# SwiGLU gate and up projections by Strassen's seven products over two token halves, with left sides made a tile ahead

## The chip, the cores and the metric

The kernel runs on one core of a Trainium2 chip. The metric is the device time of one execution in microseconds (us). A run is one execution; one more execution is recorded by the hardware profiler, and all lines of the profile come from it. The engines are PE (matrix multiplications, with its weight loads as PEld), DVE (VectorE), ACT (ScalarE), POOL (GpSimd) and SP (which here only issues transfers). Each works through its own queue of instructions in the order written and waits for others by semaphores.

## The reference

The input `x` holds 4096 tokens of 640 values. A first half (a layer norm, a Fourier transform over the tokens, two small complex matrices for each of four blocks, a shrinkage, the inverse transform, a gate) is added to `x`. The second half is the one that changes:

```python
h = _layernorm(x, axis=-1) * (1 + cb) + sb
# _B_ref(h, w_gate, w_up, w_down):
g = _silu(h @ w_gate)          # 640 x 1728
u = h @ w_up                   # 640 x 1728
x = x + gb * ((g * u) @ w_down)   # 1728 x 640
```

`cb`, `sb` and `gb` are rows of a modulation vector, and all data are float32.

## The kernel before

Every matrix product is made from two rounded parts of each factor, a high part of 12 bits and the rest: `high*high + high*low + low*high`, so three matmuls in place of one. ACT makes the high part with a copy to the rounded type, and DVE the low part with a subtraction. Everywhere below "split" means these two instructions.

The first half of the network fills the first 330 us. The last step of its inverse transform, which takes the rows `s2` from DRAM, is done in the second part: for a row of 128 tokens, `pre_c` (L991) loads and splits the spectrum row, `pre_a` (L1000) makes six matmuls of 320 columns with the matrix `gt`, adds the gated result to `x2` and takes the layer norm's statistics, `pre_x` (L1017) normalizes, and `pre_b` (L1024) transposes to `ht`, the left side with the 640 features on partitions as five slices of 128, split.

The feed-forward part runs over eight tiles of 512 tokens. For each tile:

- `split_weights` (L1037) loads 128 columns of `w_gate` or `w_up` (five slices of the 640 features) and splits them, two units ahead of their use.
- `unit` (L1094) has 27 steps: a gate and an up step for each of 13 chunks of 128 hidden features, and one for the remaining 64 of both. `proj` (L1047) makes 5 x 3 matmuls of 512 columns into one PSUM bank. A gate step ends with ACT's Silu (L1107) from the bank. An up step ends with DVE's product (L1119), and a split of it (L1120 and L1121) that gives `ah`, the left side of the down projection. No bank is added to again once it has been read.
- `down` (L1123) runs in two passes over the hidden chunks (7, then 6 and the rest), each time for four groups of 128 tokens and two halves of 320 columns. The split down weights `wdh`, `wdl` stay in SBUF throughout. A pass ends with DVE's product with the gate `gbb` (L1147) and the addition to `x2` (L1148).
- The next tile's rows are loaded and prepared between units 16 and 26, and transposed between the groups of the second pass.

The order of all instructions is written out by hand (`manual_schedule`), so the order in the text is the order of every engine's queue. Weights and rows are loaded by SP, the matrices `gt` by POOL, and outputs are stored by ACT's queue. PSUM has five names of banks, `b0`, `b1` with one bank each, and `p1`, `p2`, `p3` with two each.

Of the kernel before, what the change touches and what calls it, by code (L numbers as in the profile page):

```python
# [171 lines left out]
def body(tc, x, w1, b1, w2, b2, wg, wu, wd, c, wm, k_fa, k_tb, k_tx, k_bm, k_bx, k_ga, k_ge, k_id, out, dbg=None):  # L172
# [27 lines left out]
    with ExitStack() as top:  # L200
# [714 lines left out]

        with ExitStack() as ff:
            fp = ff.enter_context(tc.tile_pool(name="fp", bufs=1, reuse_waits="tile"))
            hts = {}
            gts = {}
            ahs = {}  # L920

            first = ExitStack()
            if dbg != "x2":
                first.enter_context(tc.manual_schedule())

            gbb = fp.tile([P, D], F32, name="gbb")
            early = {"wr": [fp.tile([P, 5, P], F32, tag="wr", bufs=4, name="wr0_0")],
                     "wh": [fp.tile([P, 5, P], F32R, tag="wh", bufs=3, name="wh0_0")]}
            gacc = fp.tile([P, D], F32, tag="chl", bufs=1, name="gacc")
            early["cr"] = [fp.tile([P, D], F32, tag="cr", bufs=2, name=f"gwm{k}") for k in range(2)]  # L930
            early["chh"] = [fp.tile([P, D], F32R, tag="chh", bufs=1, name="chh1_0")]
            wxh = fp.tile([P, D], F32R, name="wxh")
            early["wl"] = [fp.tile([P, 5, P], F32R, tag="wl", bufs=3, name="wl0_0")]
            early["xn2"] = [fp.tile([P, D], F32, tag="xn2", bufs=4, name="xn2_0_0")]
            hts[0] = fp.tile([P, 5, 2, 512], F32R, tag="ht", bufs=1, name="ht0")
            wxl = fp.tile([P, D], F32R, name="wxl")
            early["yo"] = [fp.tile([P, 320], F32, tag="yo", bufs=2, name="yo0")]
            wdh = fp.tile([P, NFC, D], F32R, name="wdh")
            wdl = fp.tile([P, NFC, D], F32R, name="wdl")

            def tile_of(shape, dt, tag, bufs, name):
                if early.get(tag):
                    return early[tag].pop(0)
                return fp.tile(shape, dt, tag=tag, bufs=bufs, name=name)


            wgv = wg.rearrange("(k p) f -> p k f", p=P)
            wuv = wu.rearrange("(k p) f -> p k f", p=P)

            gws = {}  # L950


            def gate_b(k):
                if k < 5:
                    gws[k] = tile_of([P, D], F32, "cr", 2, f"gwm{k}")
                    nc.sync.dma_start(gws[k], wm[:, 5, k, :])
                if k == 1:
                    dve.tensor_scalar(gacc, gws[0], sc[:, 0:1], None, op0=OP.mult)
                elif 1 < k < 6:
                    dve.scalar_tensor_tensor(gacc, gws[k - 1], sc[:, k - 1:k], gacc, op0=OP.mult, op1=OP.add)  # L960
                elif k == 6:
                    for hf in range(2):
                        pm = ps.tile([P, 512], F32, tag="p3", name=f"gpm{hf}")
                        mm(pm[:, :320], ones, gacc[:, 320 * hf:320 * hf + 320], start=True, stop=True)
                        act.activation(gbb[:, 320 * hf:320 * hf + 320], pm[:, :320], AF.Copy)

            def load_down(fc):
                wr = tile_of([P, D], F32, "wr", 4, f"wdr{fc}")
                if fc < NFC:
                    nc.sync.dma_start(wr, wd[128 * fc:128 * fc + 128, :])  # L970
                    h, l = wdh[:, fc, :], wdl[:, fc, :]
                else:
                    nc.sync.dma_start(wr[0:64], wd[128 * fc:F, :])
                    nc.sync.dma_start(wr[64:128], wd[128 * fc:F, :])
                    h, l = wxh, wxl
                act.activation(h, wr, AF.Copy)
                dve.tensor_tensor(l, wr, f32(h), op=OP.subtract)

            def pre_load(t):
                x2 = fx.tile([P, 4, D], F32, tag="gx", bufs=2, name=f"x2_{t}")  # L980
                nc.sync.dma_start(x2, xv[:, 4 * t:4 * t + 4, :])
                x2s[t] = x2
                gt = fp.tile([P, 4, 2, N1], F32R, tag="gt", bufs=1, name=f"gt{t}")
                pool.dma_start(gt.rearrange("p a b c -> p (a b c)"), k_ga[:, 1024 * t:1024 * t + 1024])
                gts[t] = gt
                xns[t] = []

            chs = {}
            mvs = {}

            def pre_c(t, i):  # L991
                cr = tile_of([P, D], F32, "cr", 2, f"cr{t}_{i}")
                nc.sync.dma_start(cr, s2[:, 4 * t + i, :])
                chh = tile_of([P, D], F32R, "chh", 1, f"chh{t}_{i}")
                chl = fp.tile([P, D], F32R, tag="chl", bufs=1, name=f"chl{t}_{i}")
                act.activation(chh, cr, AF.Copy)
                dve.tensor_tensor(chl, cr, f32(chh), op=OP.subtract)
                chs[t, i] = (chh, chl)

            def pre_a(t, i):  # L1000
                x2 = x2s[t]
                gt = gts[t]
                chh, chl = chs[t, i]
                for hf in range(2):
                    e = slice(320 * hf, 320 * hf + 320)
                    py = ps.tile([P, 512], F32, tag="p3", name=f"py{t}_{i}_{hf}")
                    mm(py[:, :320], gt[:, i, 0, :], chh[:, e], start=True, stop=False)
                    mm(py[:, :320], gt[:, i, 0, :], chl[:, e], start=False, stop=False)
                    mm(py[:, :320], gt[:, i, 1, :], chh[:, e], start=False, stop=True)
                    yg = tile_of([P, 320], F32, "yo", 2, f"yg{t}_{i}_{hf}")  # L1010
                    dve.tensor_tensor(yg, py[:, :320], gab[:, e], op=OP.mult)
                    dve.tensor_tensor(x2[:, i, e], x2[:, i, e], yg, op=OP.add)
                if dbg == "x2":
                    nc.sync.dma_start(ov[:, 4 * t + i, :], x2[:, i, :])
                mvs[t, i] = layer_stats(fp, x2[:, i:i + 1, :], 1, f"b{t}_{i}")

            def pre_x(t, i):  # L1017
                x2 = x2s[t]
                mv, rs = mvs[t, i]
                xn = tile_of([P, D], F32, "xn2", 4, f"xn2_{t}_{i}")  # L1020
                dve.tensor_scalar(xn, x2[:, i, :], mv[:, 0, 0:1], rs[:, 0:1], op0=OP.subtract, op1=OP.mult)
                xns[t].append(xn)

            def pre_b(t, k):  # L1024
                if k == 0 and t:
                    ht = fp.tile([P, 5, 2, 512], F32R, tag="ht", bufs=1, name=f"ht{t}")
                    hts[t] = ht
                ht = hts[t]
                pt = ps.tile([P, 512], F32, tag="p3", name=f"pt{t}_{k}")
                for i in range(4):  # L1030
                    pe.transpose(pt[:, 128 * i:128 * i + 128], xns[t][i][:, 128 * k:128 * k + 128], idn)  # L1031
# [5 lines left out]
            def split_weights(src_list, nm):  # L1037
                wr = tile_of([P, 5, P], F32, "wr", 4, f"wr{nm}")
                for dst, src in src_list:
                    nc.sync.dma_start(wr[:, :, dst], src)  # L1040
# [194 lines left out]
```

## Time and profile before

| What | Value |
|---|---|
| median of 3 runs | 1501.98 us (1499.21 to 1503.86) |
| the profiled execution: time, span | 1502.37 us, 1500.6 us |
| PE busy | 1456.5 us (97%), 8114 matmuls |
| DVE, ACT, POOL busy | 871.8, 587.7, 117.0 us (58%, 39%, 8%) |
| first transposes of the feed-forward part on PE | at 330.8 us |
| from 700 to 1100 us: PE, DVE, ACT busy | 400.0, 217.4, 114.0 us |
| moved by DMA | 179.92 MB, mean 120 GB/s |

The page gives for every group of equal instructions its busy time, the mean of one in ns, and the idle time of the engine just before them with what ended it. A view of waits adds up that idle time by who waited for whom. A timeline row gives start, duration, engine, line, operation, output and inputs, the shape, and in brackets an idle time before it with its releaser. The granted clock of PE over the span is 0.993 of full speed.

### The profile page before, as it was taken

The numbers are of one execution on the slowest core, as the hardware profiler recorded it, in microseconds if no ns is written. First come the engines' busy times: TensorE is split into PE (matmuls) and PEld (weight loads), VectorE is DVE, ScalarE is ACT, GpSimd is POOL, SyncE is SP. The second block draws the span as 40 slices with busy tenths as digits, with TensorE's granted clock in tenths as the row PEclk, the third lists the DMA queues.
The fourth block names the chain that finished last, engine by engine and source line by source line (L and its number), as shares of the span: only waits on it lengthen the run. The fifth ranks groups of instructions, "written<-read, shape, count | busy, mean of one in ns | idle before, by whom it ended". The sixth has DMA issues, their size and how long they took to land.

```text
span 1500.6 us, 20793 instructions
## 1 busy us (share of the span) xinstructions
PE 1456.5 (97%) x8114; PEld 1292.2 (86%) x8114; DVE 871.8 (58%) x1598; ACT 587.7 (39%) x1034; POOL 117.0 (8%) x215
## 2 busy tenths in 40 slices
PE   7599999989999999999999999999999999999998
PEld 2399999868989898989898989898889988898888
DVE  8478888877475437543844374447444744564433
ACT  7569989746232314231323132313231322223220
POOL 5400100030010001000100010001000100000000
PEclk9799999999999999999999999999999999999999
DMA  9946556647432423241324132513241324223210
GB/s 377 319 168 188 167 160 184 206 135 233 140 88 84 111 74 97 85 138 47 100 84 138 53 102 75 154 36 102 80 140 53 94 80 131 62 71 89 70 44 35
DMA packets 183057, 179.92 MB, mean 120 GB/s; under 512 B 19312, under 2 KB 153648, under 8 KB 180016
## 3 DMA queue, kind: packets, MB, share of 16 engines
q1 hardware_dynamic: 173728, 152.56, 34.0%
q0 software_dynamic: 3904, 14.91, 3.0%
q10 hardware_dynamic: 5328, 11.14, 2.0%
q8 instruction: 63, 1.03, 0.3%
q14 instruction: 34, 0.28, 0.1%
HBM read 137.95 MB, written 31.46 MB: 113 GB/s over the span
## 4 chain that ended last, share of the span: by engine, by line
PE 84%; DVE 5%; ACT 4%; DMA 4%; POOL 1%; SPq 1%; issue 1%; DVEq 0%; ACTq 0%; POOLq 0%
PE pd L1143 26%; PE pg L1050 8%; PE pg L1049 8%; PE pg L1051 8%; PE pu L1050 8%; PE pu L1049 8%; PE pu L1051 8%; PE pc L649 1%; PE pl L603 1%; PE pa L407 1%; DMA xx<-tt 1%; PE pb L542 1%; PE pt L1031 1%; DMA s<-xa 1%; DMA g<-s 1%
## 5 line engine op out<-in xcount | busy, mean ns | idle before, releaser
L1143 PE MATMUL pd<-wdh,ah 128*128 128x320 f32 x1664 | 384.4, 310 | 0.1
L1143 PEld LDWEIGHTS pd<-wdh,ah 128*128 128x128 f32 x1664 | 282.4, 188 | 1.0 <-DVE yo L1147 0.4
L1143 PE MATMUL pd<-wdl,ah 128*128 128x320 f32 x832 | 257.0, 309 | 0.0
L1044 DVE TENSOR_TENSOR wl<-wr,wh 128x640 fp32r<-128x640 f32 x216 | 177.5, 822 | 121.5 <-ACT wh L1043 121.5
L1050 PE MATMUL pg<-ht,wh 128*128 128x512 f32 x555 | 216.2, 389 | 0.0
L1049 PE MATMUL pg<-ht,wh 128*128 128x512 f32 x555 | 216.1, 389 | 0.0
L1051 PE MATMUL pg<-ht,wl 128*128 128x512 f32 x555 | 216.0, 389 | 0.0
L1049 PE MATMUL pu<-ht,wh 128*128 128x512 f32 x515 | 200.8, 390 | 0.0
L1050 PE MATMUL pu<-ht,wh 128*128 128x512 f32 x515 | 200.6, 390 | 0.0
L1051 PE MATMUL pu<-ht,wl 128*128 128x512 f32 x515 | 200.4, 389 | 0.0
L1107 ACT ACTIVATE sg<-pg 128x512 f32<-128x512 f32 x104 | 62.2, 598 | 336.2 <-PE pg L1051 335.3
L1120 ACT ACTIVATE ah<-sg 128x512 fp32r<-128x512 f32 x104 | 65.8, 632 | 295.4 <-DVE sg L1119 295.4
L1043 ACT ACTIVATE wh<-wr 128x640 fp32r<-128x640 f32 x216 | 157.1, 728 | 41.5 <-DVE x L1148 38.2
L1147 DVE TENSOR_TENSOR yo<-pd,gbb 128x320 f32<-128x320 f32 x128 | 62.7, 490 | 183.7 <-PE pd L1143 183.7
L1143 PEld LDWEIGHTS pd<-wdl,ah 128*128 128x128 f32 x832 | 156.3, 188 | 0.6
L1051 PEld LDWEIGHTS pg<-ht,wl 128*128 128x128 f32 x555 | 104.2, 188 | 21.8
L1119 DVE TENSOR_TENSOR sg<-pu,sg 128x512 f32<-128x512 f32 x104 | 71.7, 689 | 88.1 <-PE pu L1051 88.1
L1049 PEld LDWEIGHTS pg<-ht,wh 128*128 128x128 f32 x555 | 104.2, 188 | 21.0
L1050 PEld LDWEIGHTS pg<-ht,wh 128*128 128x128 f32 x555 | 104.2, 188 | 21.0
L1121 DVE TENSOR_TENSOR ah<-sg,ah 128x512 fp32r<-128x512 f32 x104 | 72.2, 694 | 72.7 <-ACT ah L1120 72.7
L1051 PEld LDWEIGHTS pu<-ht,wl 128*128 128x128 f32 x515 | 96.7, 188 | 20.3
L1049 PEld LDWEIGHTS pu<-ht,wh 128*128 128x128 f32 x515 | 96.7, 188 | 19.6
(209 smaller groups left out, 2001.6 us busy)
## 6 DMA issues: line engine op xcount, KB each, us to landing
wr<-in_B_w_gate_dram SPq DMA_DIRECT2D x104, 320.0 KB, 3.3
wr<-in_B_w_up_dram SPq DMA_DIRECT2D x104, 320.0 KB, 3.2
x<-in_A_x_dram SPq DMA_DIRECT2D x8, 1280.0 KB, 6.2
out_dram<-x ACTq DMA_DIRECT2D x31, 320.0 KB, 2.2
g<-s SPq DMA_DIRECT2D x28, 320.0 KB, 7.1
xx<-tt SPq DMA_DIRECT2D x56, 160.0 KB, 3.7
s<-co POOLq DMA_DIRECT2D x28, 320.0 KB, 3.4
cr<-s SPq DMA_DIRECT2D x28, 320.0 KB, 3.3
```

The lines of the kernel that those rows point to most:

```text
L407: mm(pa, fa, xnr[:, i, :, 0:128] if i < 4 else xnr[:, :, :, 128:160], start=True, stop=True)
L1043: act.activation(wh, wr, AF.Copy)
L1044: dve.tensor_tensor(wl, wr, f32(wh), op=OP.subtract)
L1049: mm(pp, wh[:, k, :], ht[:, k, 0, :], start=(k == 0), stop=False)
L1050: mm(pp, wh[:, k, :], ht[:, k, 1, :], start=False, stop=False)
L1051: mm(pp, wl[:, k, :], ht[:, k, 0, :], start=False, stop=(k == 4))
L1107: act.activation(sg, pg, AF.Silu)
L1119: dve.tensor_tensor(sg, pu, sg, op=OP.mult)
L1120: act.activation(ah[:, 0, :], sg, AF.Copy)
L1121: dve.tensor_tensor(ah[:, 1, :], sg, f32(ah[:, 0, :]), op=OP.subtract)
L1143: mm(pd[:, :320], l, m, start=(i == 0), stop=(i == len(seq) - 1))
L1147: dve.tensor_tensor(yo, pd[:, :320], gbb[:, e], op=OP.mult)
```

## The change

The tiles become 512 tokens (the first, whose left side is already there), four times 768, and 512. From the second tile on, a tile is two halves of 384 (or 256) tokens. Four of the five feature slices and two chunks of hidden features form a 2 x 2 block product, halves by features on the left and features by chunks on the right, and it is made with seven products in place of eight (Winograd's form of Strassen). The fifth slice is multiplied plainly (`fifth`). Left sums S1 to S4, and right sums T1 to T4, are needed besides the blocks themselves.

- The stages of a tile are g0 u0 s g1 d0 u1 g2 d1 u2 g3 d2 u3 g4 d3 u4 g5 d4 u5 m d5: g and u are the gate and up products for a pair of chunks, s the remaining 64 features, m the gate and up of chunk 12 together, and d the down projection for a pair, all token groups. The last d has chunk 12 and the rest in it.
- Right sums are made by POOL in the first tile, split, stored to the DRAM scratch `td` (`sum_w`, `store_t`), and loaded back for each later tile (`load_t`).
- Left sides are made row pair by row pair during the tile before (`row_*`, `pair_turn`, `pair_parts`; POOL makes the sums), each piece is split and stored to the scratch `hs`, and eight loads bring them back in the last d stage (`load_h`). `x2` goes through scratch in the same way.
- The gate is multiplied into the down weights by POOL (`fold_wd`), which are loaded and split anew for each tile; the addition to `x2` now happens in each of six d stages.
- Work of preparation is put in a list `todo` and issued in portions at `fill()` points between the products; row items are the last of the list. A row's DFT and the transposes of a pair are issued ahead of a stage's own matmuls.
- In `seven`, PE writes four banks, X, Y, Z and V. X is copied out by ACT (`keep`) after the first, the fourth and the sixth product, and PE adds on to it after each copy. `done` adds a copy to a bank and ends the gate or up value.
- Outputs are stored by SP's queue, except for the last tile.

```diff
-        FA = list(range(0, 7))
-        FB = list(range(7, 12)) + [13, 12]
-            wr = tile_of([P, 5, P], F32, "wr", 4, f"wr{nm}")
-            for k in range(5):
-                mm(pp, wh[:, k, :], ht[:, k, 0, :], start=(k == 0), stop=False)
-                mm(pp, wh[:, k, :], ht[:, k, 1, :], start=False, stop=False)
-                mm(pp, wl[:, k, :], ht[:, k, 0, :], start=False, stop=(k == 4))
-                    yo = tile_of([P, 320], F32, "yo", 2, f"yo{t}_{fcs[0]}_{g}_{hf}")
-                    dve.tensor_tensor(yo, pd[:, :320], gbb[:, e], op=OP.mult)
-                    dve.tensor_tensor(x2[:, g, e], x2[:, g, e], yo, op=OP.add)
...
+    TL = [(0, 2), (4, 3), (10, 3), (16, 3), (22, 3), (28, 2)]
+    WG = [("g", 0), ("u", 0), ("s", 0)]
+    for p in range(1, NPR):
+        WG += [("g", p), ("u", p)]
+    WG.append(("m", 0))
+    NW = len(WG)
+    STG = []
+    for n, (k, p) in enumerate(WG):
+        STG.append(("w", n))
+        if k == "g" and p:
+            STG.append(("d", p - 1))
+    STG.append(("d", NPR - 1))
...
+    def load_t(t, n):
+        if WG[n][0] == "s":
+            return
+        for i in range(2):
+            wt = take("wt", [P, 2, 2, 2, P], F32R, 2, f"wt{t}_{n}{i}")
+            nc.sync.dma_start(f32(wt.rearrange("p a b c d -> p (a b c d)")), td[n, i])
+            wts[t, n, i] = wt
...
+        def high(ks, e=slice(0, c)):
+            act.activation(wb[:, 0, ks, e], r[:, ks, e], AF.Copy)
+        def low(ks, e=slice(0, c)):
+            dve.tensor_tensor(wb[:, 1, ks, e], r[:, ks, e], f32(wb[:, 0, ks, e]), op=OP.subtract)
+        for ks in (slice(0, 2), slice(2, 5)):
+            out += [lambda ks=ks: high(ks), lambda ks=ks: low(ks)]
...
+        out = [sub(3, b12, b11), sub(1, b22, ts[:, 3]), sub(0, b22, b12), sub(2, b21, ts[:, 1])]
+        for i in range(2):
+            wt = take("wt", [P, 2, 2, 2, P], F32R, 2, f"wt0_{n}{i}")
+            wts[0, n, i] = wt
+            src = ts[:, 2 * i:2 * i + 2]
+            def high(wt=wt, src=src):
+                act.activation(wt[:, :, 0], src, AF.Copy)
+            def low(wt=wt, src=src):
+                dve.tensor_tensor(wt[:, :, 1], src, f32(wt[:, :, 0]), op=OP.subtract)
+            out += [high, low]
+        return out
+    def store_t(n):
+        for i in range(2):
+            if (0, n, i) in wts:
+                nc.sync.dma_start(td[n, i], f32(wts[0, n, i].rearrange("p a b c d -> p (a b c d)")))
...
+    def fold_wd(t, p):
+        w = wdraw[t, p]
+        for f in range(2):
+            pool.tensor_tensor(w[:, f], w[:, f], gbb, op=OP.mult)
...
+    def row_split(r):
+        chh = take("pc", [P, D], F32R, 4, f"chh{r}")
+        chl = take("pc", [P, D], F32R, 4, f"chl{r}")
+        act.activation(chh, crs[r], AF.Copy)
+        dve.tensor_tensor(chl, crs[r], f32(chh), op=OP.subtract)
+        chs[r] = (chh, chl)
...
+        sa_ = take("pc", [P, 2, 2, P], F32, 4, f"sa{t}_{i}")
+        sb_ = take("pc", [P, 2, 2, P], F32, 4, f"sb{t}_{i}")
+        S1, S2, S3, S4 = sa_[:, 0], sa_[:, 1], sb_[:, 0], sb_[:, 1]
+        out = []
+        def tt(o, a, b, op):
+            return lambda: pool.tensor_tensor(o, a, b, op=op)
+        out += [tt(S1, A[1][0], A[1][1], OP.add), tt(S3, A[0][0], A[1][0], OP.subtract),
+                tt(S2, S1, A[0][0], OP.subtract), tt(S4, A[0][1], S2, OP.subtract)]
+        pieces = [[A[0][0], A[0][1]], [A[1][1], h32[:, 4]], [S1, S2], [S3, S4]]
+        for j, src in enumerate(pieces):
+            ho = {}
+            def high(j=j, src=src, ho=ho):
+                o = fp.tile([P, 2, 2, 2, P], F32R, tag="ho", bufs=2, name=f"ho{t}_{i}_{j}")
+                ho[0] = o
+                for b in range(2):
+                    act.activation(o[:, b, :, 0], src[b], AF.Copy)
+            def low(j=j, src=src, ho=ho):
+                o = ho[0]
+                for b in range(2):
+                    dve.tensor_tensor(o[:, b, :, 1], src[b], f32(o[:, b, :, 0]), op=OP.subtract)
+            def store(j=j, ho=ho):
+                nc.sync.dma_start(
+                    hsd[t][:, 2 * j:2 * j + 2, :, :, 128 * i:128 * i + 128].rearrange(
+                        "p a b c d -> p (a b c) d"),
+                    f32(ho[0].rearrange("p a b c d -> p (a b c) d")))
+            out += [high, low, store]
...
+    def load_h(t):
+        n = P * TL[t][1]
+        for j in (0, 6, 1, 3, 5, 2, 4, 7):
+            hb[t, j] = take(f"h{j}", [P, 2, 2, n], F32R, 1, f"h{t}_{j}")
+            nc.sync.dma_start(f32(hb[t, j].rearrange("p a b c -> p (a b c)")),
+                              hsd[t][:, j].rearrange("p a b c -> p (a b c)"))
...
+        bk = [bank(q, f"pw{t}_{n}_{q}")[:, :N] for q in range(4)]
+        X, Y, Z, V = bk
+        def prod(b, a, w, start=False):
+            w = W[w]
+            for kp in range(2):
+                mm(b, w(0, kp), a[:, kp, 0], start=start and kp == 0, stop=False, skip_group_check=not start)
+                mm(b, w(0, kp), a[:, kp, 1], start=False, stop=False, skip_group_check=not start)
+                mm(b, w(1, kp), a[:, kp, 0], start=False, stop=kp == 1, skip_group_check=not start)
+        def fifth(b, half, f):
+            c = slice(P * f, P * f + P)
+            mm(b, wb[:, 0, 4, c], AK[:, half, 0], start=False, stop=False, skip_group_check=True)
+            mm(b, wb[:, 0, 4, c], AK[:, half, 1], start=False, stop=False, skip_group_check=True)
+            mm(b, wb[:, 1, 4, c], AK[:, half, 0], start=False, stop=True, skip_group_check=True)
+        def keep(b, nm):
+            s = take("s", [P, N], F32, 5, f"s{t}_{n}_{nm}")
+            act.activation(s, b, AF.Copy)
+            return s
+        def done(a, f, b, s):
+            dve.tensor_tensor(s, b, s, op=OP.add)
+            if k == "g" or (k == "m" and f == 0):
+                sg = take("sg", [P, N], F32, 4, f"sg{t}_{n}_{a}{f}")
+                sgs[a, f] = sg
+                act.activation(sg, s, AF.Silu)
+                return
+            if k == "m":
+                o = take(f"ra{a}", [P, 2, N], F32R, 1, f"a12_{t}_{a}")
+                sg, fc = sgs[a, 0], 12
+            else:
+                o = take(f"a{2 * a + f}", [P, 2, N], F32R, 1, f"a{t}_{p}_{a}{f}")
+                sg, fc = sgs[a, f], 2 * p + f
+            acts.setdefault((t, fc), {})[a] = o
+            dve.tensor_tensor(sg, s, sg, op=OP.mult)
+            split_act(t, fc, sg, o[:, 0], o[:, 1])
+        prod(X, A11, "B11", True)
+        s1 = keep(X, "x")
+        prod(V, S3, "T3", True)
+        s7 = keep(V, "v")
+        fill()
+        prod(Y, A12, "B21", True)
+        fifth(Y, 0, 0)
+        fill()
+        done(0, 0, Y, s1)
+        prod(X, S2, "T2")
+        s2_ = keep(X, "y")
+        fill()
+        prod(V, A22, "T4")
+        fifth(V, 1, 0)
+        prod(X, S1, "T1")
+        s3 = keep(X, "z")
+        done(1, 0, V, s2_)
+        fill()
+        prod(Z, S4, "B22", True)
+        fifth(Z, 0, 1)
+        done(0, 1, Z, s3)
+        fifth(X, 1, 1)
+        done(1, 1, X, s7)
+        fill()
...
+                                mm(pd[g, hf][:, :320], l, m, start=(i == 0), stop=(i == len(q) - 1))
+                        if part:
+                            e = slice(320 * hf, 320 * hf + 320)
+                            x2 = x_row(t, g)
+                            dve.tensor_tensor(x2[:, e], x2[:, e], pd[g, hf][:, :320], op=OP.add)
...
+        for i in range(H):
+            a, b = r0 + i, r0 + H + i
+            s = 2 + 5 * i if H == 3 else 3 + 6 * i
+            parts = []
+            at(s, 1, lambda a=a: row_load(a))
+            at(s + 1, 1, lambda a=a: row_split(a))
+            at(s + 1, 1, lambda b=b: row_load(b))
+            at(s + 2, 0, lambda a=a: row_dft(a))
+            at(s + 2, 1, lambda b=b: row_split(b))
+            at(s + 3, 1, lambda a=a: row_norm(a))
+            at(s + 3, 0, lambda b=b: row_dft(b))
+            at(s + 4, 1, lambda b=b: row_norm(b))
+            at(s + 5, 0, lambda i=i: pair_turn(t, i))
+            at(s + 5, 0, lambda i=i, parts=parts: parts.extend(pair_parts(t, i)))
+            for j in range(10):
+                at(s + 5, 1, lambda j=j, parts=parts: parts[j]())
+            for j in range(10, 16):
+                at(s + 6, 1, lambda j=j, parts=parts: parts[j]())
+        return steps
...
+            if what == "w":
+                c = flat.index((t, n))
+                if c + 2 < len(flat):
+                    (after.append if t == 0 else lambda f: f())(lambda: load_w(*flat[c + 2]))
+                if c + 1 < len(flat):
+                    a = flat[c + 1]
+                    if a[0]:
+                        (after.append if t == 0 else lambda f: f())(lambda: load_t(*a))
+                    todo += prep_w(*a)
...
+            todo += rows.get((si, 1), ())
+            per_fill = max(1, -(-len(todo) // 6))
+            def fill():
+                for _ in range(per_fill):
+                    if todo:
+                        todo.pop(0)()
+            if what == "d":
+                if n == NPR - 1 and t + 1 < NT:
+                    load_h(t + 1)
+                down(t, n, fill)
+            elif t == 0:
+                plain(n, fill)
+            elif WG[n][0] == "s":
+                rest(t, n, fill)
+            else:
+                seven(t, n, fill)
+            while todo:
+                todo.pop(0)()
+            if t == 0 and (what, n) == ("w", NW - 1):
+                held, after = after, []
+            elif t == 0 and (what, n) == ("d", NPR - 1):
```

## The prediction

> **What bounds the kernel now.** I read the page's slices first, then the costliest groups, the waits after 342 us, and the timeline of TensorE and of the two evicting engines.
>
> ```profile
> PE   7599999989999999999999999999999999999998
> DVE  8478888877475437543844374447444744564433
> L1143 PE MATMUL pd<-wdh,ah 128*128 128x320 f32 x1664 | 384.4, 310 | 0.1
> L1050 PE MATMUL pg<-ht,wh 128*128 128x512 f32 x555 | 216.2, 389 | 0.0
> L1044 DVE TENSOR_TENSOR wl<-wr,wh 128x640 fp32r<-128x640 f32 x216 | 177.5, 822 | 121.5 <-ACT wh L1043 121.5
> L1148 DVE TENSOR_TENSOR x<-x,yo 128x320 f32<-128x320 f32 x128 | 63.0, 492 | 4.4
> ```
>
> From slice 9 of 40 on TensorE is full, and its gate, up and down matmuls have no idle time before them (0.0, 0.1). Between 342 us and the end the view of waits names no wait of PE's matmuls at all. So TensorE's issue sets the time, and VectorE (DVE) is about half busy. A matmul's duration overlaps the next one's, so its price is the distance of starts:
>
> ```profile
> 799.66 0.39 PE L1051 MATMUL pu<-ht,wl 128*128 128x512 f32 x1
> 799.89 0.39 PE L1049 MATMUL pu<-ht,wh 128*128 128x512 f32 x1
> ...
> 850.35 0.31 PE L1143 MATMUL pd<-wdl,ah 128*128 128x320 f32 x1
> 850.50 0.46 PE L1143 MATMUL pd<-wdh,ah 128*128 128x320 f32 x2
> ```
>
> That is 0.227 us for 512 columns and 0.147 for 320; the 256-column matmuls of L603 start 0.119 apart. The straight line gives 0.174 for 384 (estimate). Check: 8 tiles x (405 x 0.227 + 328 x 0.147) + 28 rows x (6 x 0.147 + 5 transposes x 0.109, L1031) = 1161, and the feed-forward part runs on PE from 330.8 to 1496.8 = 1166 us. The sum below is made against the span of 1500.6, with 1.8 outside it (1502.37); that run is 0.4 above the median, so nothing is corrected for it.
>
> **Term 1, matmuls removed: -47.** In the changed instruction order a pair of hidden chunks takes 54 matmuls (7 products x 6 and 4 x 3 for the fifth slice) in place of 60, each over half the tile's tokens. Tile 0 keeps the old 140.2. Tiles 1 to 4 (768 tokens): 13 x 54 + 30 = 732 x 0.174 + 492 x 0.147 = 199.7 each. Tile 5 (512 tokens): 732 x 0.119 + 328 x 0.147 = 135.3. Sum 1074 against 1121. Rows and transposes keep their count (40).
>
> **Term 2, what the seven products make TensorE wait for: +188.** The bank X is evicted three times in one stage, and PE adds into it again only when ScalarE (ACT) has copied it. Before, no bank was taken up again. ACT and DVE work strictly in the written order, so that copy stands behind whatever was queued earlier:
>
> ```profile
> 807.57 0.69 DVE L1119 TENSOR_TENSOR sg<-pu,sg 128x512 f32<-128x512 f32 x1 [1.32 <-PE pu L1051]
> 808.30 0.63 ACT L1120 ACTIVATE ah<-sg 128x512 fp32r<-128x512 f32 x1 [2.90 <-DVE sg L1119]
> 808.96 0.69 DVE L1121 TENSOR_TENSOR ah<-sg,ah 128x512 fp32r<-128x512 f32 x1 [0.70 <-ACT ah L1120]
> ```
>
> Here one chain runs DVE, ACT, DVE with 0.04 between them, and DVE stands 0.70 while ACT rounds. After the change each u stage has four chains add, multiply, (ACT) round, subtract. DVE: 320 columns 0.49 and 512 columns 0.69 give 0.556 for 384; ACT 0.54 (from 0.632 and 0.728); its PSUM copy 0.50 (from 0.435 for 320, L705, and 0.615 for 512, L418). A chain is 3 x 0.556 + 0.54 + gaps = 2.3.
>
> *A u stage by hand*, from its first matmul: X done 1.0, V 2.1, Y 3.6, X again 4.7, V 6.3, X 7.3, Z 8.9, end 9.4; a result is readable 0.2 later. DVE: weights' first low part 3.4 to 4.0, chain of Y to 6.3, of V 6.4 to 9.0, second low part to 9.9, of Z to 12.1, of the last X to 14.4. So DVE and ACT end 5.1 us after PE. In the next g stage ACT can copy X only behind the last rounding, at 14.2; PE wants it at 9.4 + 3.6 = 13.0: 1.3 lost, and 0.5 more at the second copy. **u then g: 1.8.** A d stage in between drains this.
>
> *Row work placed at a stage's end.* A row's split or norm is the last item of its stage, and its DFT or transposes are the first matmuls of the next; PE waits for DVE's whole backlog. By stage, for a 768-token tile that prepares six rows:
> - s to g1: 1.0 (chain of the rest); g1 itself 0.3
> - g1 to d0: add, Silu, split on ACT 0.74, on DVE 0.82, after PE's end: 2.7. The same g3 to d2: 2.7
> - u1 to g2: 1.8; g2 to d1 (norm 0.61 behind the last add): 1.3
> - u2 to g3: two pieces of left sides (1.7 on DVE) and a split (0.8) on top of the 5.1: 7.7, of it 0.8 inside u2
> - u3 to g4: norm behind the backlog, 5.7; in g4 four weight splits queue ahead of the first eviction: 2.4
> - u4 to g5: split behind the backlog: 5.9
> - u5 to m: the same four splits in u5, 3.1; m's first two copies behind the backlog, 4.4
>
> Together 39; three tiles 117. Tile 4 prepares four narrower-tile rows: by the same items 26. Tile 5 (no rows, but stages of 54 x 0.119 = 6.4 us against unchanged weight splits): 0.7 in each u, 1.7 + 2.2 in the g behind it, with m 28. Tile 0 has plain 512-column groups and eight banks in turn, so only its row work counts, behind a backlog of 2 to 3 us: 17. DVE's sum for a 768-token tile, about 165 us of some 247, shows that no engine is full; it is the order that costs. Bounds: DVE's starts can follow 0.06 to 0.1 before the former end, which shortens each backlog by about 1 (term 2: 130); half as much again if each stop also delays the next (280).
>
> Folding the gate into the down weights takes away L1147 (128 x 0.49 on DVE) but adds up six times into x2 where it was twice: 72 x 0.49 a tile. Beside PE's 12 x 0.88 in a d stage it is hidden: nothing.
>
> **Term 3, reloading: +7.** Left sides come back as eight loads of 768 KB in the last d stage. At the 377 GB/s of the first slice that is 2.1 us each, 17 together. Tiles 1 to 4 have a d stage of 19.4 over it: hidden (up to 3 a tile if the last store is late). Tile 0's is only 12.9, and behind its output stores the first weight sums wait too: 7. All transfers of the feed-forward part are some 270 MB, over 1300 us 210 GB/s.
>
> **Term 4, GpSimd beside VectorE: +5.** One place of the trace shows both with two SBUF inputs:
>
> ```profile
> 326.06 0.49 DVE L868 TENSOR_TENSOR x<-x,cl 128x320 f32<-128x320 f32 x1
> 326.11 1.17 POOL L868 TENSOR_TENSOR x<-x,acc 128x320 f32<-128x320 f32 x1
> ```
>
> The second comer, GpSimd, took 1.17 where its other rows at L868 took 0.86. After the change GpSimd multiplies 14 x 640 columns and makes 12 sums of 256 in a tile: with 0.86 for 320 and 0.19 for one element that is 1.53 and 0.72 each, 31 us. Delayed GpSimd work lies off the path, VectorE delayed has not been seen: I take 5, between 0 and the second rival's 87. The Trainium skill, SBUF — State Buffer, section "Who interferes with whom", says that a VectorE instruction with two SBUF inputs and a GpSimd one that reads SBUF exclude each other, and whoever issues second blocks fully; the trace agrees for the one side (0.31 more). By that rule the sum is the second rival's.
>
> A stop also touches PE's clock: after the wait of 13.9 us at 51 us, fourteen matmuls of L542 took 3.3 us, 0.214 apart in place of 0.112. My stops are 1 to 8 us, for which no row shows it: nothing taken, up to 15 (three stops over 5 us in each of three tiles, 1.65 each). The Trainium skill, TensorE: Matmul & The Clock Gate, Part 1, puts the loss at an idle window of about 3.4 us; by it the sum would have those 15 in it.
>
> **Sum.** 1500.6 - 47 + 188 + 7 + 5 = 1653.6, and 1.8 outside: **1655**.
>
> **Rivals.**
> *PE stays full.* DVE's and ACT's averages have room, and the extension of the ring to two sets of banks hides the stops. Then only term 1: 1455. For it: not one wait of PE now. Against it: the backlog of 5.1 follows from the written order, and PE needs the copy 3.6 into a stage. It decides if all stops together are under 47, 9 a tile.
> *GpSimd blocks VectorE (slower still).* DVE has 85 us of two-SBUF-input work in a tile of 247, so 31 x 0.34 = 11 us meet; tile 0 (GpSimd also makes 52 weight sums, 68 us, beside 0.53) 36; tile 5, 8. All of it on VectorE and passed on to PE: 43 + 36 + 8 = 87, so 1737. From 68 down it is inside my forecast's neighbourhood.
> *Transfers bound it.* 270 MB at 200 GB/s is 1350 us for this part, 1686 in all. For it: 512-byte pieces in the left sides' stores, one SP queue whose loads wait in order. Against it: 188 GB/s at a DMA share of 0.64 means some 294 possible.
>
> **Chances.** Forecast 0.62, PE full 0.13, GpSimd 0.14, transfers 0.08, the remaining 0.03 about no change. Term 2 from 130 to 280 alone gives 1597 to 1747; the lower end reaches further, to 1550, towards the first rival. Range 1550 to 1745. A measurement can't tell 0.3% here, which I count as the same: faster 0.13, same 0.03, slower 0.84.
>
> **What would show it.** PE's matmul idle time should be some 200 us, ended by ACT's copy of X (the second product into X), and by DVE for py and pt. Term 1 is right if 384 columns start 0.174 apart. DVE should be near 70% busy. If 256-wide or 384-wide starts are longer, or PE's waits name DMA, the terms are wrong; if GpSimd's neighbours on DVE are longer than 0.556, the second rival has it.

## The result and the profile after

The changed kernel takes 1901.97 us (median of 4, 1900.3 to 1914.59) against 1502.74 for the kernel before (median of 4 in the same series): a ratio of 1.268, 95% interval 1.2622 to 1.2738. I had forecast 1655, with a range of 1550 to 1745. The direction was right and the size was far off: the time is 157 us beyond the range. The profiled execution has a span of 1900.0.

These are rows of the changed kernel's page: the slices of PE, GpSimd and PE's granted clock, two groups, and the chain by engine.

```profile
PE   7699999777675877888877888877889788887778
POOL 4301003344231021121021121021121021200111
PEclk9899999998887888999888999988899899999999
L1466 PE MATMUL pd<-wdh,a 128*128 128x320 f32 x1712 | 398.5, 316 | 14.9 <-ACT wdh L1098 14.1
L1350 PE MATMUL pw<-h,wt 128*128 128x384 f32 (+1 forms) x520 | 185.2, 356 | 119.1 <-ACT s_y L1362 68.6
PE 43%; DVE 22%; ACT 14%; DMA 10%; issue 6%; POOL 3%; SPq 2%; ACTq 0%; DVEq 0%; POOLq 0%
```

From slice 10 on PE now shows 7 and 8 in nearly every slice where it showed 9; its granted clock is no longer full; and of the chain that ends last PE holds 43% where it held 84%. The view of PE's waits from 330 us on, which before had no line for its matmuls after 342 us (us in total, times, longest):

```profile
PE py L1152 <- ACT chh L1142: 86.0, 19, 12.3
PE pw L1350 <- ACT s_y L1362: 68.6, 34, 6.3
PE pt L1177 <- DVE xn L1164: 31.8, 8, 7.6
PE pw L1350 <- DMA wt<-td: 30.2, 5, 17.4
PE py L1153 <- DVE chl L1143: 22.3, 19, 3.4
PE pw L1350 <- ACT s_x L1362: 19.6, 14, 2.8
PE pd L1466 <- ACT wdh L1098: 14.1, 2, 13.1
PE pw L1350 <- ACT wb L1025: 11.9, 8, 1.9
```

`py` and `pt` are the row work at a stage's start, `s_x` and `s_y` the copies of X, `wt` the reloaded weight sums, `wb` and `wdh` the splits of the gate or up weights and of the down weights.

**Where the 400 us are.** For each pair of neighbouring matmuls from 330 us on I took the distance of their starts, less what the first one's width takes at full clock (0.227, 0.174, 0.147, 0.119, 0.110 us for 512 to 128 columns). Where the second has idle time before it, the excess counts as a stop; the rest is called slow clock: of the 106 us in the changed kernel, 103 lie where the granted clock is 0.50, and 87 are matmuls at about twice the distance. Before: 1164 of work and 2 of everything else. After: 1116 of work, 344 of stops, 106 of slow clock. So -48 + 342 + 106 = 400. All kernels in this table were taken apart in the same way. Their feed-forward part begins between 328 and 332 us, so the work of kernels with the same matmuls differs by up to 3. The last column is the time by which DVE's instructions exceeded the median of their kind, of those over 1.2 times it.

| Kernel | time | work | stops | slow clock | DVE overlong |
|---|---|---|---|---|---|
| before | 1502 | 1164 | 2 | 0 | 0 |
| changed | 1902 | 1116 | 344 | 106 | 77 |
| e1: row items first | 1857 | 1118 | 294 | 109 | 70 |
| e2: gate folded once | 1837 | 1117 | 289 | 95 | 13 |
| e3: copies of X ahead | 1820 | 1117 | 265 | 103 | 58 |
| e5: e1, e2 and e3 | 1716 | 1115 | 197 | 67 | 19 |
| e8: tile 0's order | 1877 | 1115 | 318 | 107 | 84 |
| e10: e2, e3, e8, list issued early | 1616 | 1116 | 120 | 44 | 22 |
| e4: eight products | 1722 | 1180 | 160 | 47 | 51 |
| e7: e4 and gate folded once | 1687 | 1180 | 134 | 37 | 18 |
| e11: e7, e8, list issued early | 1599 | 1180 | 64 | 19 | 27 |

**One stop in full**, the boundary from u2 to g3 of tile 1, from the changed kernel's timeline. First PE: the stop and what follows.

```profile
700.81 0.34 PE L1358 MATMUL pw<-h,wb 128*128 128x384 f32 x1
705.49 0.64 PE L1152 MATMUL py<-chh,gt 128*128 128x320 f32 x1 [4.34 <-ACT chh L1142]
708.20 0.64 PE L1153 MATMUL py<-chl,gt 128*128 128x320 f32 x1 [2.07 <-DVE chl L1143]
...
709.70 0.52 PE L1350 MATMUL pw<-h,wb 128*128 128x384 f32 x1
710.02 0.52 PE L1351 MATMUL pw<-h,wb 128*128 128x384 f32 x1
...
711.94 0.34 PE L1351 MATMUL pw<-h,wt 128*128 128x384 f32 x1
712.11 0.34 PE L1352 MATMUL pw<-h,wt 128*128 128x384 f32 x1
```

Then ACT, DVE and GpSimd in the same stretch.

```profile
702.08 0.52 ACT L1282 ACTIVATE a<-sg 128x384 fp32r<-128x384 f32 x1 [1.07 <-DVE sg L1380]
704.29 0.52 ACT L1282 ACTIVATE a<-sg 128x384 fp32r<-128x384 f32 x1 [1.69 <-DVE sg L1380]
704.72 0.72 ACT L1142 ACTIVATE chh<-cr 128x640 fp32r<-128x640 f32 x1
...
704.85 0.56 DVE L1283 TENSOR_TENSOR a<-sg,a 128x384 fp32r<-128x384 f32 x1 [0.59 <-ACT a L1282]
705.32 0.75 DVE L1210 TENSOR_TENSOR ho<-sb,ho 128x256 fp32r<-128x256 f32 x2
705.99 2.15 DVE L1143 TENSOR_TENSOR chl<-cr,chh 128x640 fp32r<-128x640 f32 x1
...
705.86 3.69 POOL L1089 TENSOR_TENSOR wdr<-wdr,gbb 128x640 f32<-128x640 f32 x2 [20.70 <-DVE ho L1210]
```

Three causes meet here: the order of the queues, GpSimd beside DVE, and the clock. PE is done with the stage at 701. ACT and DVE still run the last chains, and the row's split `chh` stands behind them, until 705.44. The subtraction `chl` then takes 2.15 us, because GpSimd started to multiply the gate in 0.13 before. And when PE resumes, its 384-column matmuls start 0.32 apart, not 0.17, until 711.9: the granted clock is 0.50 from 705.1 to 711.9.

### The profile page after: what moved, and what is told of

The parts are those of the page before. It is cut to its first block, busy times and chain, and to the rows that moved or that the text cites. A ratio compares the mean times of both kernels' runs of the same rounds, so it can differ in the third digit from the quotient of the medians.

```text
span 1900.0 us, 24357 instructions
## 1 busy us (share of the span) xinstructions
PE 1545.8 (81%) x8939; PEld 1443.1 (76%) x8939; DVE 1179.3 (62%) x2165; ACT 778.6 (41%) x1578; POOL 349.3 (18%) x433
## 4 chain that ended last, share of the span: by engine, by line
PE 43%; DVE 22%; ACT 14%; DMA 10%; issue 6%; POOL 3%; SPq 2%; ACTq 0%; DVEq 0%; POOLq 0%
PE pd L1466 17%; PE pw L1350 5%; PE pw L1352 4%; PE pw L1351 4%; DVE wb L1028 4%; DVE sg L1380 3%; ACT a L1282 2%; DVE wdl L1099 2%; DVE a L1283 2%; DMA wdr<-in_B_w_down_dram 2%; ACT wb L1025 2%; PE pc L649 2%; DMA wt<-td 2%; DMA h<-hs 1%; DVE chl L1143 1%
## 5 line engine op out<-in xcount | busy, mean ns | idle before, releaser
L1466 PE MATMUL pd<-wdh,a 128*128 128x320 f32 x1712 | 398.5, 316 | 14.9 <-ACT wdh L1098 14.1
L1089 POOL TENSOR_TENSOR wdr<-wdr,gbb 128x640 f32<-128x640 f32 x84 | 142.1, 1710 | 1001.8 <-DMA wdr<-in_B_w_down_dram 751.0
L1466 PEld LDWEIGHTS pd<-wdh,a 128*128 128x128 f32 x1712 | 298.8, 194 | 16.5 <-ACT wdh L1098 15.1
L1350 PE MATMUL pw<-h,wt 128*128 128x384 f32 (+1 forms) x520 | 185.2, 356 | 119.1 <-ACT s_y L1362 68.6
L1466 PE MATMUL pd<-wdl,a 128*128 128x320 f32 x888 | 279.9, 316 | 2.5 <-DVE wdl L1099 2.1
L1028 DVE TENSOR_TENSOR wb<-r,wb 128x512 fp32r<-128x512 f32 (+3 forms) x173 | 160.4, 937 | 190.3 <-ACT wb L1025 183.4
L1470 DVE TENSOR_TENSOR x<-x,pd 128x320 f32<-128x320 f32 x384 | 180.7, 485 | 139.3 <-PE pd L1466 138.0
L1350 PEld LDWEIGHTS pw<-h,wt 128*128 128x128 f32 x520 | 104.7, 201 | 137.6 <-ACT s_y L1362 82.1
L1352 PE MATMUL pw<-h,wt 128*128 128x384 f32 (+1 forms) x520 | 177.5, 341 | 0.0
L1351 PE MATMUL pw<-h,wt 128*128 128x384 f32 (+1 forms) x520 | 177.0, 340 | 0.0
L1466 PEld LDWEIGHTS pd<-wdl,a 128*128 128x128 f32 x888 | 171.9, 194 | 5.6 <-DVE wdl L1099 5.5
L1350 PE MATMUL pw<-h,wb 128*128 128x384 f32 (+1 forms) x390 | 140.2, 359 | 12.7 <-ACT wb L1025 11.9
L1352 PE MATMUL pw<-h,wb 128*128 128x384 f32 (+1 forms) x390 | 138.8, 356 | 2.7 <-DVE wb L1028 2.1
L1351 PE MATMUL pw<-h,wb 128*128 128x384 f32 (+1 forms) x390 | 137.2, 352 | 0.0
L1351 PEld LDWEIGHTS pw<-h,wt 128*128 128x128 f32 x520 | 105.3, 203 | 0.0
L1352 PEld LDWEIGHTS pw<-h,wt 128*128 128x128 f32 x520 | 104.5, 201 | 0.0
L1356 PE MATMUL pw<-h,wb 128*128 128x384 f32 (+1 forms) x260 | 88.5, 340 | 8.2 <-ACT s_z L1362 8.2
```

Source lines behind the costliest of these rows:

```text
L1028: dve.tensor_tensor(wb[:, 1, ks, e], r[:, ks, e], f32(wb[:, 0, ks, e]), op=OP.subtract)
L1089: pool.tensor_tensor(w[:, f], w[:, f], gbb, op=OP.mult)
L1350: mm(b, w(0, kp), a[:, kp, 0], start=start and kp == 0, stop=False, skip_group_check=not start)
L1351: mm(b, w(0, kp), a[:, kp, 1], start=False, stop=False, skip_group_check=not start)
L1352: mm(b, w(1, kp), a[:, kp, 0], start=False, stop=kp == 1, skip_group_check=not start)
L1356: mm(b, wb[:, 0, 4, c], AK[:, half, 0], start=False, stop=False, skip_group_check=True)
```

## The experiments

Each edit is against the changed kernel unless said otherwise, and each was executed once. The four executions of the changed kernel lie within 15 us of each other, three of them within 2, so a difference of a few us decides nothing. Line numbers shift by a few in some kernels.

**e1, row items first.**

```diff
-                    todo += rows.get((si, 1), ())
+                    todo[:0] = rows.get((si, 1), ())
```

> One edit: the row items are put at the head of a stage's list of preparation work in place of its end. Theory (a row's split or norm is late because it stands behind the stage's own evictions on ACT and DVE): PE's waits at py and pt, 140 us in the changed kernel, fall below 60, half-clock matmuls fall with them, time about 1785. Rival (the backlog as such is the cause, and only moves): the waits for the copies of X rise by as much as py and pt fall, time above 1870.

Measured 1857, between the two. The waits at py and pt all but vanish (`chh` from 86.0 to 4.8, `xn` from 31.8 to 0.5), but the stops did move, only not to X. PE's waits in e1:

```profile
PE pd L1466 <- ACT wdh L1098: 65.3, 16, 16.0
PE pw L1352 <- DVE wb L1028: 62.6, 25, 5.7
PE pw L1350 <- ACT s_y L1362: 29.8, 22, 3.7
PE pw L1350 <- ACT wb L1025: 21.2, 7, 4.1
PE pd L1466 <- DVE wdl L1099: 19.6, 30, 1.6
```

The splits of weights, now last in the list, are late instead. This suggests that what stands at the end of a stage is late, whatever it is; e10 tests it.

**e2, gate folded once.**

```diff
+            wdd = nc.dram_tensor("wdd", (NPR + 1, P, 2, D), F32, kind="Internal").ap()
...
+                if t:
+                    nc.sync.dma_start(w, wdd[p])
...
             def fold_wd(t, p):
+                if t:
+                    return
...
+                if t == 0:
+                    out.append(lambda: nc.sync.dma_start(wdd[p], w))
```

> The gate is multiplied into the down weights by GpSimd in tile 0 only and stored to scratch; later tiles load the product, so 70 of 84 GpSimd multiplications of 1.58 us go. Theory (GpSimd shuts out DVE's instructions with two SBUF inputs): DVE's overlong instructions, 77 us in the changed kernel, fall below 35, and the time by 40 to 60 to about 1850. Rival (GpSimd is off the path): within 15 of 1902.

Measured 1837, 65 less, and DVE's overlong instructions fall from 77 to 13. The row split shows it best. For the tile `chl` on DVE, minimum, median and maximum in ns, the changed kernel has

```profile
L1143 DVE TENSOR_TENSOR chl<-cr,chh x28: 812/826/2154, 374.7 to 1596.9; 128x640 fp32r<-128x640 f32 x28
```

and e2

```profile
L1150 DVE TENSOR_TENSOR chl<-cr,chh x28: 812/824/826, 372.5 to 1555.6; 128x640 fp32r<-128x640 f32 x28
```

The stops fall by 55 and the slow clock by 11; together that is a little more than the theory's 40 to 60. PE waits less for `s_y` (44.6 in place of 68.6) and for `chl` (7.3 in place of 22.3), which both hang on DVE's chains, but not for the split of the folded weights themselves (`wdh`, 14.2 in place of 14.1). So it is the delay of DVE that costs, and not a late fold. By its busy share (18%) GpSimd looked off the path, and it cost 65 us all the same.

**e3, copies of X ahead of the roundings.**

```diff
-                done(0, 0, Y, s1)
                 prod(X, S2, "T2")
                 s2_ = keep(X, "y")
+                done(0, 0, Y, s1)
...
                 s7 = keep(V, "v")
+                flush()
...
-                    split_act(t, fc, sg, o[:, 0], o[:, 1])
+                    if f:
+                        late.append(lambda: split_act(t, fc, sg, o[:, 0], o[:, 1]))
+                    else:
+                        split_act(t, fc, sg, o[:, 0], o[:, 1])
```

> In a u stage the second copy of X is issued on ACT before the first eviction, and the last two roundings are issued after the next stage's first two copies. Theory (the copies of X stand behind the evictions' roundings): PE's waits for s_x, s_y and s_z, 96 us in the changed kernel, fall below 30, time about 1810. Rival (the queue's order hardly counts, ACT and DVE are simply behind): these waits fall but those at py and pt rise by as much, time above 1870.

Measured 1820. The wait for `s_y` falls from 68.6 to 11.1 and `s_x` leaves the list; `s_z`, the third copy, rises from 8.2 to 44.0, so the sum is not under 30 as expected. The waits at py and pt do not rise: `chh` 55.7, `chl` 26.8, `xn` 26.3, together 109 against 140. So the order of ACT's queue is a cause of its own, as the theory has it. The moved line stands in the code of all stages with seven products, so the g and m stages changed with the u stages.

**e4, eight products on the same scaffold.**

```diff
-                prod(X, A11, "B11", True)
-                s1 = keep(X, "x")
...
+                for f in range(2):
+                    for a in range(2):
+                        b = bk[2 * f + a]
...
+                            l = ((A11, A12), (S1, A22))[a][kk % 2]
...
+                            mm(b, l, m, start=(i == 0), stop=(i == len(seq) - 1))
```

> Eight products in place of seven on the changed kernel's tiles, stages, loads and stores, each value in its own bank over 15 matmuls, evicted from the bank (the left sum S1 stands in for the block that is not stored, so the output is not the reference's). PE gets 6 matmuls more in each of 13 stages, 63 us. Theory (scaffold and products share the loss: row work, down weights split anew, GpSimd): the copies' waits of 96 vanish with some clock loss, time about 1830. Rival (the seven products with their banks taken up again cause nearly all of it): below 1650.

Measured 1722: 180 us faster with 64 us more of matmuls (1180 against 1116). So on this scaffold the seven products lose 244 us, in stops (184) and clock (59), to save 64. That is between theory and rival: the products' share is larger than I thought. The eight products also take 155 us off DVE's busy time and 111 off ACT's, since nothing is copied out and added. The scaffold itself loses the other 220 against the kernel before: 16 of work from narrower matmuls, 158 of stops and 47 of clock.

**e5, the three edits together.**

> The three edits together: row items first, gate folded once, copies of X ahead of roundings. Alone they gave 45, 65 and 82 us. Theory (three separate causes of stops): they add, near 1710. Rival (one backlog of DVE and ACT that shows up at the next waiting place): less than the best pair, above 1770.

Measured 1716, that is 186 of the 192 that the edits gave alone. The times add, as the theory has it; their parts do not. The stops fall by 147, where the edits alone took 50, 55 and 79 (184 together), and the slow clock falls by 39, where it changed by 11 in all. So the stops of the three overlap a little, and the fewer they are, the more of the clock comes back. The largest waits that are left are for the weight splits (`wdh` 55.0, `wb` 31.8 and `wdl` 29.5), put last by e1.

**e6, idle matmuls in the stops.**

```diff
+                    for _ in range(20):
+                        mm(b[:, :256], curwb[0][:, 0, 4, 0:P], curwb[0][:, 0, 0, :], start=True, stop=True)
```

> Twenty idle matmuls of 256 columns (2.4 us) into a bank that the next matmul starts anew, before the row work at five stages of each of three tiles where PE stopped 1 to 8 us. Theory (PE's clock is halved for 3.4 us after a stretch of 3.4 us in which PE was busy less than half): idle time falls by some 36, filled by as much idle work, and the half-clock excess of 87 falls to about 65, time 1870 to 1890. Rival (the clock falls for another reason than idleness): the excess stays within 5 of 87, and the time at 1900 or above.

Measured 1895. Stops fall by 39 to 305 and work rises by 36, as expected; slow clock falls from 106 to 102 only (the expectation's 87, the matmuls at about twice the distance, to 81), and the mean granted clock rises from 0.914 to 0.922. The sign is the theory's, the size is the rival's: inconclusive, and the reason for e9 and e12.

**e7, eight products with the gate folded once** (e4's and e2's edits).

> Eight products as before (1722) with the gate folded into the down weights once only. Theory (GpSimd's multiplications shut out DVE, which is on PE's path): as much as in the seven-product kernel, 50 to 65, near 1665. Rival (with less DVE work there is room for it): under 25, above 1697.

Measured 1687, a gain of 35 where the seven products gained 65, between theory and rival. DVE's overlong time falls by 33 here and by 64 in e2, so both times the gain is about the delay that is taken off DVE. With the eight products DVE has fewer instructions that GpSimd can meet, but GpSimd is not free there either.

**e8, tile 0's order.** Tile 0 alone lost 74 us to stops, where I had expected 17. How one of them (12.3 us at 433 us) comes about is in the changed kernel's timeline:

```profile
413.38 2.62 SPq L1213 DMA_DIRECT2D hs<-ho  x2
...
417.84 0.44 SPq L1079 DMA_DIRECT2D wdr<-in_B_w_down_dram  x1
...
423.16 3.01 POOL L1089 TENSOR_TENSOR wdr<-wdr,gbb 128x640 f32<-128x640 f32 x2 [13.13 <-DMA wdr<-in_B_w_down_dram]
426.15 0.71 POOL L1050 TENSOR_TENSOR ts<-r 128x256 f32<-128x256 f32 x1
...
428.37 1.31 ACT L1059 ACTIVATE wt<-ts 128x512 fp32r<-128x512 f32 x2 [19.02 <-POOL ts L1050]
...
432.25 0.72 ACT L1142 ACTIVATE chh<-cr 128x640 fp32r<-128x640 f32 x1
```

SP issues the down weights late, behind stores of left sides that wait for DVE's part of their split. GpSimd stands 13.13 us waiting for them, with the weight sums queued behind. ACT stands 19.02 us for the sums, with the row's split queued behind. And PE waits for the split. Four queues, each in order, pass one late transfer on.

```diff
+                            elif p:
+                                todo.append(lambda p=p: fold_wd(0, p))
...
+                            if t == 0:
+                                for f in held:
+                                    f()
                             load_h(t + 1)
```

> Tile 0 alone: GpSimd makes a stage's weight sums ahead of the fold of down weights, and the next tile's first weight loads are issued before the output stores. Theory (in tile 0 the fold waits for its load on SP, the sums behind it on GpSimd, ACT behind the sums, PE behind ACT; stops of 12.3, 11.6, 13.1 and 17.4): the time falls by 30 to 45 to about 1865. Rival (the loads are late in themselves): within 10 of 1902.

Measured 1877, 25 less. The stops of 11.6 and 17.4 are gone and that of 12.3 is now 8.0; the one of 13.1, for the down weights' split, stays. Less than expected, but more than the rival allowed. In tile 0 itself the stops fall only from 74 to 60, and in e10 they are still 53, so this shows the cause of a part of them, and what causes the rest was not tested.

**e9 and e12, stops of known length in the kernel before.**

```diff
+                for _ in range(PAUSE[t, n]):
+                    act.activation(scr, lastpu[0][:, 0:P], AF.Copy)
+                mm(pg[:, 0:P], scr, scr, start=True, stop=True)
```

> The kernel before, with two stops of PE of a known kind in each of tiles 1 to 7: ACT copies 128 columns of the last up bank 4 to 28 times in a row, and one small matmul on the result stands ahead of the next gate unit. Stops of about 1.2 to 7 us, 45 in all. Theory (the clock is halved for 3.4 us after a stretch of 3.4 us with PE busy less than half): stops over 5 us are always followed by matmuls 0.45 apart, stops of 2 to 5 us often, stops under 1.7 us never; time near 1502 + 45 + 15. Rival (only a wholly idle stretch of 3.4 us counts): no stop under 3.4 us is followed by slow matmuls.

> As the run with the stops of PE in the kernel before, but the ACT copies are issued ahead of the up step's eviction and are 2 to 9, so that the stops are some 0.7 to 3 us (the base of the other run was 1.9, each copy 0.31). Theory (half clock follows a stretch of 3.41 us in which PE was busy less than about 0.54): no stop under 1.5 us is followed by matmuls 0.45 apart; of those from 1.7 to 3 us, those are that lie with over 1.57 us in one stretch. Rival (a stop must come near 3.4 us): none of them.

In e9 all 14 stops were longer than meant, 3.16 to 10.6 us, 83 in all, because an eviction and a weight split stood ahead of the copies on ACT. Every one was followed by 6 to 12 matmuls more than 0.4 us apart, also that of 3.16, the only one which could speak against the rival; the time was 1615, that is 83 of stops, 28 of slow clock and 2 of added matmuls above the kernel before. In e12 the 14 stops were 0.68 to 2.84 us. None of the seven up to 1.60 us was followed by slow matmuls; of the two of 1.91, one; of the five from 2.22 to 2.84, four. Here are a stop of 1.60 and one of 1.91 of e12, each with the matmuls after it:

```profile
941.21 0.33 PE L1113 MATMUL pg<-scr 128*128 128x128 f32 x1 [1.60 <-ACT scr L1104]
...
941.89 0.40 PE L1051 MATMUL pg<-ht,wl 128*128 128x512 f32 x1
942.13 0.40 PE L1049 MATMUL pg<-ht,wh 128*128 128x512 f32 x1
...
1091.62 0.33 PE L1113 MATMUL pg<-scr 128*128 128x128 f32 x1 [1.91 <-ACT scr L1104]
...
1092.29 0.63 PE L1051 MATMUL pg<-ht,wl 128*128 128x512 f32 x1
1092.71 0.63 PE L1049 MATMUL pg<-ht,wh 128*128 128x512 f32 x1
```

After the first, 512 columns start 0.23 apart; after the second 0.43, for 3.4 us. The rival falls: a stop need not come near 3.4 us. The theory holds but for its limit: 1.60 us of the longer stop that had no effect (2.53) lay in one step of the clock (busy 53%), and by the theory the clock should have fallen.

**e10 and e11, the list issued early.**

```diff
-                    per_fill = max(1, -(-len(todo) // 6))
+                    per_fill = max(1, -(-len(todo) // 3))
```

> The changed kernel with gate folded once, copies of X ahead of roundings, tile 0's two edits, and the list of preparation issued in three portions in place of six, so that it is out before a stage's last evictions, in its old order. Theory (what stands at the end of a stage is late, whatever it is): PE's waits at py, pt, wdh, wdl and wb stay under 80 together (138 in the three edits together, 1716), time 1630 to 1670. Rival (the same work ahead of the evictions delays these, and PE waits for X instead): above 1700.

> Eight products (S1 standing in for the block that is not stored) with gate folded once, tile 0's two edits and the list in three portions. PE's work is 1180 of matmul starts, so 1515 without a stop. Theory (the scaffold's own loss is order, in tile 0 above all): 1610 to 1640, 50 to 75 below 1687. Rival (its loads and stores bound it): above 1670.

e10 measured 1616, 286 us below the changed kernel with the same arithmetic on PE. In its view of waits `chh` has 12.1, `wdh` 13.8 and `xn` 7.9; the largest is `s_y` again with 22.1. e11 measured 1599, both better than expected. If e2, e3 and e8 add (65, 82 and 25), some 114 of e10's 286 are left for the list; alone it was not run. With the order mended on both sides the eight products are still 17 us faster than the seven, although they have 64 us more of matmuls: stops are 56 fewer and slow clock is 25 less. Of e11's 64 us of stops 52 lie in tile 0, so from tile 1 on the eight products hardly stop (12), and the seven do (68). No version beat the kernel before.

## Why the prediction was right in kind and wrong in size

The direction was right, and so were the matmuls saved and the places of the steady tiles' stops. Three steps failed: the clock was taken at nothing and cost 106, GpSimd's delay of DVE was taken at 5 and cost about 65 (11 of them clock), and tile 0's stops were taken at 17 and are 74.

- **Term 1 (-47)** was right: work is 1116 against 1164, -48, and 384 columns start 0.174 apart.
- **Term 2, steady tiles (39 each)**: the stops are where I put them, and the large ones of tile 1 nearly as long. Predicted and measured there: u2 to g3 7.7 and 7.0, g1 to d0 2.7 and 2.8, g3 to d2 2.7 and 3.3, u3 to g4 with g4 itself 8.1 and 9.2, u4 to g5 5.9 and 6.9, u5 to m 7.5 and 6.1; u1 to g2 1.8 and 4.1. With the small ones, tiles 1 to 3 lose 51 (tile 1's 68 less its wait for the weight sums), 57 and 59, tiles 4 and 5 45 and 40 where I had 26 and 28. Part of the agreement is luck, since the forecast of these stops had no GpSimd in it: the five largest (u1 to g2, u2 to g3, u3 to g4, u4 to g5, u5 to m) are 33 together where I had 31, but 25 in e2, without the folds. DVE's busy time is as I had it: 1179 us, 71% of 1655.
- **Term 2, tile 0 (17)** failed: 74. I counted only its row work "behind a backlog of 2 to 3 us", and did not follow the fold, the sums and the split through SP, GpSimd and ACT, one behind the other (e8). **Term 3 (+7)** was too small for the same queue: the first weight sums behind tile 0's output stores cost 17.4 alone.
- **Term 4 (+5)** failed. The row of 1.17 for 0.86 was the hint, and I took almost nothing since "VectorE delayed has not been seen". It could not be seen: before, GpSimd had hardly anything to multiply. e2 puts it at 65 for 70 of the 84 folds, and DVE's overlong time is 77, near the 87 of my second rival; that rival's 1737 was still 165 too low. The Trainium skill, SBUF — State Buffer, section "Who interferes with whom", calls the contention an exclusive lock; the 2.15 for 0.82 above agrees.
- **The clock ("nothing taken, up to 15")** failed worst: 106. I found no row with a short stop that slowed PE, and took the absence as no cost. But the trace of the kernel before has one, 3 us behind the matmuls that I read:

```profile
71.51 1.78 PE L542 MATMUL pb<-tb,g 128*128 128x128 f32 x8 [1.69 <-DVE z L550]
72.94 0.99 PE L603 MATMUL pl<-z,w1a 128*128 128x256 f32 x3
```

After this stop of 1.69 the granted clock is 0.50 from 71.86 to 75.27, and the 256-column matmuls of L603 start 0.21 apart in place of 0.119. e12 shows the same for a stop of 1.91 in an otherwise full stream, and the changed kernel has dozens of such stops.

- The sum of stops was 200 in the forecast (terms 2 to 4) and 344 in the trace. Of the 144 missing, tile 0 has 57 and tile 1's first loads 11; the other 76 lie in tiles 1 to 5, where e2 takes away 51. With the 106 of clock that is 250, against 247 between 1655 and 1902.
- The transfers' rival did not come: the mean is 181 GB/s, and its waits are single late loads (`wt`, five times).

## What to carry to other kernels

Fewer multiplications pay only if the engines that feed and empty the array get no longer chains: here 10% fewer matmuls in one stage needed a bank to be copied out three times, and every copy stood in a queue behind evictions that waited for another engine. When such a trade is made, write down for each engine's queue what stands last in a stage and who needs it first in the next; then move the list forward before judging the arithmetic (with e2, e3 and e8 that took 286 us off here). Price a stop of the array by its length plus what a halved clock takes after it, and price GpSimd's two-input work as DVE's.

## What the hardware showed that I had not expected

- **The clock falls after short stops.** In e12 no stop up to 1.60 us halved PE's clock; the shortest that did was 1.91, and the longest that did not 2.53. The granted clock changes in steps of 3.41 us on a fixed grid. By that grid each of the five falls in e12 followed a step in which PE was busy at most 44% by the profile. Two steps of 53% brought no fall: one holds the whole stop of 1.60 shown above, the other 1.60 of the stop of 2.53, which lay across a boundary, as did the stop of 1.91 that had no effect. In the changed kernel, from 340 us on, 50 falls followed steps of at most 53.5%, and five steps of 51 to 54% brought none, so the limit is near one half. The stops of a step add up: four of these falls came after steps with two to four stops, none of them over 1.42. One step at half clock costs up to 1.7 us, and one fall can bring several: the 50 falls brought 90 steps. The Trainium skill, TensorE: Matmul & The Clock Gate, Part 1, names an idle window of about 3.4 us as the condition; the step's length agrees, but it need not be idle, and the measurement decides.
- **GpSimd's multiplication holds DVE up nearly to its own end**: `chl`, started 0.13 after one of 1.6 us, took 2.15 in place of 0.82.
- **Issuing is not free on SP**: in the changed kernel's timeline two stores of the left sides' pieces, 512 KB each in 512-byte pieces, took SP 2.62 us from 413.38 on, the first row shown under e8. What waits behind them on SP starts that much later.
